# Spreading the softmax with two whole products and a block transposition, contracting two chunks per matmul, loading weight tails from GpSimd, and a remade order

## The chip, the cores and the metric

The kernel runs on one core of one Trainium2 chip, in one launch. The metric is device time in microseconds, the median of several executions: 495.63 us before the change (three runs, 494.08 to 496.65).

A core has five engines with an instruction stream each: TensorE (PE) multiplies matrices, VectorE (DVE), ScalarE (ACT) and GpSimd (POOL) do elementwise work, SyncE (SP) issues transfers. 16 DMA engines move data between HBM and the on-chip SBUF, and they serve the transfers of all issuing engines. Matmuls write to PSUM; from there DVE or ACT copies results to SBUF (an *eviction*).

## What is computed

The reference is a decode step with its gradients. Two tokens (batch 2, one position, width 576) are normalised; a grouped-query attention over a cache of 4096 keys and a gated linear unit are added to the input; then come the gradients of everything.

```python
def _A_ref(x, k_cache, v_cache, wq, wo):          # B=2, D=576, Hq=32, Hkv=16, Sk=4096, Dh=128
    q = (x @ wq).reshape(B, 1, Hq, Dh).transpose(0, 2, 1, 3)
    k, v = repeat(k_cache, 2, axis=1), repeat(v_cache, 2, axis=1)
    p = softmax(einsum("bhqd,bhkd->bhqk", q, k) * Dh ** -0.5)
    o = einsum("bhqk,bhkd->bhqd", p, v)
    return o.transpose(0, 2, 1, 3).reshape(B, 1, Hq * Dh) @ wo

def _B_ref(x, w_gate, w_up, w_down):              # F = 4608
    return ((x @ w_gate) * (x @ w_up)) @ w_down

xn = layernorm(A_x)
out = A_x + _A_ref(xn, k_cache, v_cache, wq, wo) + _B_ref(xn, w_gate, w_up, w_down)
# returned: out and the gradients by A_x, k_cache, v_cache, wq, wo, w_gate, w_up, w_down
```

All arrays are bf16. The two caches are 2 x 16 x 4096 x 128, 32 MiB each (1 MiB for each batch entry and head), and their gradients are as large. The weights are some 25 MB, and their gradients too. So every input is read once, every gradient is written once: 92.48 MB in, 92.48 MB out.

## The kernel before

The work is cut into 16 steps `s`: two key/value heads and one batch entry each. A step loads 2 MiB of keys and 2 MiB of values as tiles of 128 partitions x 8 KB, transposes each on DVE into a tile `X` (four-byte pairs in 32 x 32 blocks), multiplies it with the queries (`score`), takes the softmax, *spreads* the probabilities into two layouts, and uses them twice: for the contraction with the cache (`contract`) and for outer products that are the cache's gradient (`head_outer`), evicted and stored 1 MiB at a time. Values take part with the probabilities `pp`, keys with the gradient of the scores `dd`. Between the steps lie eight groups of `wq`/`wo` columns and nine slices of the gated unit.

Sixteen big tiles of 8 KB per partition serve for everything large; each use has a cap:

```python
NBIG, NGU, NWW, NBD = 16, 1, 5, 3
CAP = {"kv": 9, "X": 7, "st": 4}      # loaded caches, transposed copies, output tiles that wait for their store
KVSTORE = "SP"
```

The order of the instructions is made when the program is built: the class `Order` keeps a clock for every engine and every DMA line, with a written cost for each operation, and issues what can start first, by priority. On the chip each engine then works through its own stream in just that order, waiting on semaphores. So a written cost or a priority does no work on the chip, but it decides the order of the streams, which engine gets an eviction, and which tile is used next.

Spreading, 32 small products of 32 x 32 results each, then one eviction:

```python
def spread(src, dst_ps):
    for c4 in range(4):
        for a in range(4):
            blk, rows = src[:, 32 * c4:32 * c4 + 32], identP[:, 32 * a:32 * a + 32]
            nc.tensor.matmul(dst_ps[32 * a:32 * a + 32, 32 * c4:32 * c4 + 32], lhsT=blk, rhs=rows, ...)
    for a in range(4):
        for c4 in range(4):
            ...                       # the same with lhsT and rhs exchanged, into columns 128 to 255
# in softmax(s), and the same for dd in dscore(s):
spread(c["pr"], m_t[m])
e = yield EV(256)                     # ACT or DVE
cp(e, pp_t[S["pp"]][:].rearrange("p t n -> p (t n)"), m_t[m][:, 0:2 * P])
yield REL("m", m)
```

Contraction, 64 products of 128 columns in four column groups of the array, then a fold:

```python
for part in range(2):
    for k in range(8 * part, 8 * part + 8):
        for j in range(4):
            c, l = k + NCH // 2 * (j // 2), j % 2
            nc.tensor.matmul(ct[32 * j:32 * j + 32, 0:P], lhsT=view(rT, 0, P, 4 * c + 2 * l, [[1, 32]]),
                             rhs=kv_t[kvS[s][t][l]][:, Dh * c:Dh * (c + 1)],
                             start=(k == 0), stop=(k == NCH // 2 - 1))
for l in range(G):
    yield REL("kv", kvS[s][t][l])
...                                   # evict 128 columns to osb, one matmul with fold, copy to oT
```

Outer products: each 1 MiB store needs four evictions of 128 x 1024:

```python
i = yield ACQ("st")                   # an output tile
for k in range(2):
    nc.tensor.matmul(o[:, k, :], lhsT=pr2[32 * c4:32 * c4 + 32, :],
                     rhs=BD[32 * c4:32 * c4 + 32, 8 * l + 4 * h2:8 * l + 4 * h2 + 4, :], ...)
cp(e, view(st[:], 0, P, 2048 * A + 512 * h2, [[1024, 2], [1, 512]]), o[:])
```

The last 64 of the 576 rows of `wq`, `w_gate` and `w_up` (the *tails*) are loaded from SP, whose stream also holds every load of the caches and every store of their gradients:

```python
yield DMA("SP", 0.45, 128 * 256 * 2, 512)
nc.sync.dma_start(ww_t[w][:, 4 * FS:WB], A_wq[512:576, n0:n0 + FS].rearrange("p (h n) -> h p n", h=2))
...
yield DMA("SP", 0.45, 64 * FS * 2, 1024)
nc.sync.dma_start(gu[64 * w:64 * w + 64, 8 * FS:9 * FS], Wsrc[512:576, f0:f0 + FS])
```

Of the kernel before, what the change touches and what calls it, by code (L numbers as in the profile page):

```python
# [13 lines left out]
P = 128  # L14
# [20 lines left out]
class Landing:  # L35
    def __init__(self, work, packet):
        self.work, self.packet, self.t = work, packet, None
# [6 lines left out]
class Lines:  # L44
    def __init__(self):
        self.now, self.line = 0.0, ([], [])

    def run(self, until=None):
        while (self.line[0] or self.line[1]) and (until is None or self.now < until):
            busy = [q for q in self.line if q]  # L50
            total = sum(q[0].packet for q in busy)
            step, first = min(((q[0].work * total / q[0].packet, k) for k, q in enumerate(busy)))
            ends = until is None or step <= until - self.now
            step = step if ends else until - self.now
            for q in busy:
                q[0].work -= step * q[0].packet / total
            self.now += step
            for q in busy:
                if q[0].work < 1e-9 or ends and q is busy[first]:
                    q[0].t = self.now + 1.4  # L60
                    q.pop(0)

    def push(self, k, at, work, packet):
        self.run(at)
        if not (self.line[0] or self.line[1]):
            if at > self.now + 0.3:
                work += DRY
            self.now = max(self.now, at)
        item = Landing(work, packet)
        self.line[k].append(item)  # L70
        now, line, left = self.now, self.line, [[(x, x.work) for x in q] for q in self.line]
        self.line = tuple(list(q) for q in line)
        self.run()
        self.now, self.line = now, line
        for q in left:
            for x, w in q:
                x.work = w
        return item


class Order:

    HOP = 0.12
    def __init__(self):
# [4 lines left out]
        self.quad = None  # L89
# [48 lines left out]
    def start(self, s):  # L138
        r = s.req
        if r[0] == "op":  # L140
            return max(s.ready, self.free[r[1]]), r[1]
# [25 lines left out]
    def run(self):  # L167
        while self.streams:
# [12 lines left out]
            if r[0] in ("op", "any"):  # L181
                cost = r[2] if r[0] == "op" else next(c for x, c, _ in r[1] if x == e)
                quad = r[3] if len(r) > 3 else None
                if quad is not None and self.quad == (1 - quad, t):
                    cost = 0.12
                self.free[e] = t + cost
                if e == "PE":
                    self.quad = (quad, t + cost)
                s.ready = t + cost + self.HOP
# [24 lines left out]
def PE(cost):  # L214
    return ("op", "PE", 0.9 * cost)
# [14 lines left out]
def EV(cols):  # L230
    return ("any", [("ACT", 0.19 + cols * 0.00083, 0.0), ("DVE", 0.16 + cols * 0.00104, cols / 1024 * BIAS)])

# [25 lines left out]
def DMA(engine, cost, nbytes, row=8192):  # L258
# [6 lines left out]
CAP = {"kv": 9, "X": 7, "st": 4}  # L265
MLP0, MLPD = 7, 3.04
KVSTORE = "SP"
WQ0, WO0 = -3, 0
LATENCY, DRY = {"SP": 0.6, "ACT": 0.6, "POOL": 2.0}, 0.4
BIAS = 0.39  # L270
SLACK = {"PE": 0, "ACT": 0.24, "DVE": 0.42, "POOL": 8.48, "SP": 2.18}
STEP = 28.0
HEAD = {"turn0": 32.8, "turn1": 5.6, "att": 18.2, "dsc": -4.1, "con": 20.2, "out1": 32.0, "out0": -0.1, "front": 136.3, "back": 186.6, "W0": -106.9, "W1": 1.4, "load": -18.7}
TAIL = {"turn0": -311.6, "att": -941.4, "dsc": 107.7, "conv": -25.4, "out1": 360.1, "out0": 2.8, "front": 14.6, "back": -0.1, "W0": 72.9, "W1": 0.3, "BD0": -350.1, "load": -45.9}
PR = {"turn0": 159.1, "turn1": 503.5, "att": -177.4, "dsc": -354.1, "conv": 107.5, "con": 255.2, "out1": 239.8, "out0": 221.8,
      "front": -254.4, "back": -141.0, "W0": -80.5, "W1": 16.3, "BD1": 432.8, "BD0": -175.2, "mlp": 0.4, "wout": -413.4,
      "store": 556.3, "load": 796.4, "wload": -183.0, "fin": -239.5, "const": -134.5, "mload": 817.1}
# [8 lines left out]
def kernel(  # L286
# [30 lines left out]
    G = 2  # L317
# [47 lines left out]
    osb_t = tiles("osb", 2, [P, P])  # L365
    od.ring("ch", 2)
    ch_t = []
    for i in range(2):
# [6 lines left out]
            cr=const.tile([P, 1], FP32, name=f"cr{i}"), ds=const.tile([P, P], BF16, name=f"ds{i}")))  # L375
# [66 lines left out]
    fold = const.tile([P, GH], BF16, name="fold")  # L442
    foldf = const.tile([P, GH], FP32, name="foldf")
# [9 lines left out]
    def consts():  # L453
# [17 lines left out]
        yield DVE(0.2)  # L471
        sums(foldf[:].rearrange("p (l r) -> p l r", l=2), [[32, 2], [1, 2], [64, 2]])
# [19 lines left out]
    def front():  # L492
# [23 lines left out]
        yield PE(0.8)  # L516
# [11 lines left out]
        for src, dst in ((yb, dyr), (xnb, xnr)):  # L528
            i = yield ACQ("o")
            o = o_t[i]  # L530
            yield PE(0.6)
# [28 lines left out]
        yield PE(1.0)  # L560
# [52 lines left out]
    def put(engine, parts, tag, slot, events=()):  # L613
        def run():
            for j, (dst, src, nbytes) in enumerate(parts):
                yield DMA(engine, 0.77 if engine == "POOL" else 0.45, nbytes)
# [6 lines left out]
    def unit(mms, pe, cols, ev, store, quad=None):  # L623
        i = yield ACQ("o")
        yield PE(pe) if quad is None else ("op", "PE", pe, quad)
# [6 lines left out]
    def cols_unit(A, rhs, st, off):  # L632
# [10 lines left out]
        return mms, 0.6, 1024, ev  # L643

    def rows_unit(j, lhs, st):
# [10 lines left out]
        return mms, 0.35, D, ev  # L656

    def rows_outer(lhs, dst, p, events=()):
# [3 lines left out]
        store = Store(FC, put("POOL", [(dst, src, 128 * FC * D * 2)], "st", i, events), p)  # L662
# [3 lines left out]
    def cols_outer(rhs, dst, p, events=()):  # L666
# [3 lines left out]
        store = Store(2, put("POOL", [(dst, src, 128 * 4 * FS * 2)], "st", i, events), p)  # L670
# [3 lines left out]
    def tail_outer(rhss, dsts, p, events=()):  # L674
# [4 lines left out]
        store = Store(2, put("POOL", parts, "tl", i, events), p)  # L679

        def mk(A):
# [9 lines left out]
            return mms, 0.3, 256, ev  # L691
# [8 lines left out]
    def mlp(i, Lgu, Ld, gs_slot, wd_slot):  # L700
# [7 lines left out]
        yield PE(1.3)  # L708
# [19 lines left out]
        yield PE(2.2)  # L728
# [30 lines left out]
        yield PE(0.4)  # L759
# [9 lines left out]
        yield PE(0.75)  # L769
# [21 lines left out]
        yield PE(1.5)  # L791
# [17 lines left out]
    def group_front(g):  # L809
# [7 lines left out]
        yield PE(0.75)  # L817
# [12 lines left out]
        def replicate(t):  # L830
            m = yield ACQ("m")
            rp = m_t[m][:, 0:8 * GH].rearrange("p (e k) -> p e k", e=4)
            yield PE(0.35)
# [17 lines left out]
        yield PE(2.2)  # L851
# [18 lines left out]
    def group_back(g):  # L870
# [8 lines left out]
        yield PE(0.4)  # L879
# [15 lines left out]
        yield PE(0.75)  # L895
# [12 lines left out]
        yield PE(0.4)  # L908
# [14 lines left out]
        yield PE(0.8)  # L923
# [27 lines left out]
    def load_kv():  # L951
        n = 0
        for s in range(NS):
            g, b = divmod(s, Bq)
            yield PRIO(pr("load", s))
            for t in range(2):
                for l in range(G):
                    i = yield ACQ("kv")
                    yield DMA("SP", 0.45, 1 << 20)
# [6 lines left out]
    def load_w(item):  # L966
        kind, i = item
        if kind in ("wq", "wo"):
# [3 lines left out]
            if kind == "wq":  # L972
                yield DMA("SP", 0.45, 128 * 256 * 2, 512)
                nc.sync.dma_start(ww_t[w][:, 4 * FS:WB],
                                  A_wq[512:576, n0:n0 + FS].rearrange("p (h n) -> h p n", h=2))
# [10 lines left out]
        else:  # L986
# [4 lines left out]
            for w, Wsrc in enumerate((B_w_gate, B_w_up)):  # L991
# [3 lines left out]
                yield DMA("SP", 0.45, 64 * FS * 2, 1024)  # L995
                nc.sync.dma_start(gu[64 * w:64 * w + 64, 8 * FS:9 * FS], Wsrc[512:576, f0:f0 + FS])
            yield ("lset", Lgu)
            d = yield ACQ("ww")
            yield DMA("SP", 0.45, 128 * FC * D * 2, 4608)
# [40 lines left out]
    def build_BD():  # L1040
        for s in range(NS):
            g, b = divmod(s, Bq)
            for t in (1, 0):
# [5 lines left out]
                yield PE(0.2)  # L1049
# [26 lines left out]
    def spread(src, dst_ps):  # L1076

        for c4 in range(4):
            for a in range(4):
                blk = src[:, 32 * c4:32 * c4 + 32]  # L1080
                rows = identP[:, 32 * a:32 * a + 32]
                nc.tensor.matmul(dst_ps[32 * a:32 * a + 32, 32 * c4:32 * c4 + 32], lhsT=blk, rhs=rows,
                                 start=True, stop=True)
        for a in range(4):
            for c4 in range(4):
                blk = src[:, 32 * c4:32 * c4 + 32]
                rows = identP[:, 32 * a:32 * a + 32]
                nc.tensor.matmul(dst_ps[32 * c4:32 * c4 + 32, P + 32 * a:P + 32 * a + 32], lhsT=rows, rhs=blk,
                                 start=True, stop=True)

    def head_outer(s, t, l, pr2, done):
# [7 lines left out]
        def mk(A, h2):  # L1099
# [9 lines left out]
            return mms, 0.45, 1024, ev  # L1109
# [24 lines left out]
    def softmax(s):  # L1134
# [6 lines left out]
        for l in range(G):  # L1141
            yield PE(0.95)
# [275 lines left out]
```

## Time and profile before

| what | before |
|---|---|
| time, median of 3 runs | 495.63 us |
| span of the profiled execution | 493.5 us |
| busy: PE, DVE, ACT, POOL | 393.3, 362.6, 323.4, 228.2 us |
| moved by DMA | 186.20 MB, mean 377 GB/s |
| share of the 16 DMA engines' time: queue of SP, queue of GpSimd | 71.7%, 23.6% |
| granted TensorE clock, mean | 0.623 of full speed |

How to read it: a *group* of the page is a line of the kernel with one engine and one kind of operands; it has the busy time, the mean duration and the idle time just before its instructions, with what ended that idle time. Lines 392 and 394 are the helper `cp` on ACT and on DVE, line 388 is the helper `t32` (DVE transposition), line 617 issues stores, 960 loads the caches, 974 and 996 load tails, 1070 is `score`, 1082 and 1088 `spread`, 1103 `head_outer`, 1248 `contract`, 1058 builds the block-diagonal operand `BD` on GpSimd. *SPq* is the issuing stream of SP. Stretches are given in us from the span's start.

### The profile page before, as it was taken

The numbers are of one execution on the slowest core, as the hardware profiler recorded it, in microseconds if no ns is written. First come the engines' busy times: TensorE is split into PE (matmuls) and PEld (weight loads), VectorE is DVE, ScalarE is ACT, GpSimd is POOL, SyncE is SP. The second block draws the span as 40 slices with busy tenths as digits, with TensorE's granted clock in tenths as the row PEclk, the third lists the DMA queues.
The fourth block names the chain that finished last, engine by engine and source line by source line (L and its number), as shares of the span: only waits on it lengthen the run. The fifth ranks groups of instructions, "written<-read, shape, count | busy, mean of one in ns | idle before, by whom it ended". The sixth has DMA issues, their size and how long they took to land.

```text
span 493.5 us, 19375 instructions
## 1 busy us (share of the span) xinstructions
PE 393.3 (80%) x8522; PEld 255.6 (52%) x8522; DVE 362.6 (73%) x662; ACT 323.4 (66%) x490; POOL 228.2 (46%) x323
## 2 busy tenths in 40 slices
PE   1549759989888987667799788988878888798886
PEld 0436525556564555545555556546555456455543
DVE  7658848878875797664687788876878498778872
ACT  6027766768746877435587757776828686787682
POOL 6153453619480531327176747350547237472311
PEclk9957755565655579565755766555555566756765
DMA  7999899999999999999999999999999999998864
GB/s 269 403 382 399 307 371 382 419 415 404 360 390 419 373 330 419 410 404 406 348 374 308 408 421 406 388 418 387 346 419 395 419 423 423 400 420 362 320 266 180
DMA packets 34236, 186.20 MB, mean 377 GB/s; under 512 B 4156, under 2 KB 6344, under 8 KB 17768
## 3 DMA queue, kind: packets, MB, share of 16 engines
q1 hardware_dynamic: 22224, 141.25, 71.7%
q0 software_dynamic: 11920, 43.72, 23.6%
q8 instruction: 66, 1.08, 0.8%
q14 instruction: 18, 0.15, 0.1%
q10 hardware_dynamic: 8, 0.00, 0.0%
HBM read 92.48 MB, written 92.48 MB: 375 GB/s over the span
## 4 chain that ended last, share of the span: by engine, by line
PE 40%; DMA 24%; DVE 11%; issue 9%; ACT 8%; POOL 5%; SPq 2%; ACTq 0%; POOLq 0%; DVEq 0%
DMA out_dram<-big 16%; PE ps_o L1103 9%; ACT big L392 7%; PE ps_m L1248 7%; PE ps_m L1070 7%; DMA ww<-in_A_wq_dram 6%; DVE big L388 5%; POOL BD L1058 4%; DVE big L394 3%; DMA ww<-in_A_wo_dram 3%; PE ps_o L651 2%; PE ps_o L637 2%; PE ps_m L854 2%; PE ps_m L731 1%; PE ps_m L595 1%
## 5 line engine op out<-in xcount | busy, mean ns | idle before, releaser
L392 ACT CAST big<-ps_o 128x1024 bf16<-128x1024 f32 (+1 forms) x302 | 271.8, 953 | 63.6 <-PE ps_o L1103 38.4
L388 DVE STREAM_TRANSPOSE big<-big 128x1024 f32<-128x1024 f32 x128 | 155.8, 1228 | 16.8 <-DMA out_dram<-big 8.4
L1058 POOL TENSOR_TENSOR BD<-vr,mask 128x2048 bf16<-128x2048 bf16 x32 | 115.3, 3603 | 65.0 <-DVE vr L394 38.4
L394 DVE CAST big<-ps_o 128x1024 bf16<-128x1024 f32 (+1 forms) x74 | 82.6, 1117 | 17.5 <-PE ps_o L1103 7.4
L1070 PE MATMUL ps_m<-big,W 128*32 128x128 bf16 x2048 | 64.2, 295 | 7.0 <-issue 3.7
L1103 PE MATMUL ps_o<-BD,pp 32*128 32x512 bf16 x256 | 55.5, 536 | 8.2 <-ACT big L392 4.9
L1070 PEld LDWEIGHTS <-W 128*32 128x32 bf16 x2048 | 49.7, 131 | 20.6 <-issue 18.5
L1103 PE MATMUL ps_o<-BD,dd 32*128 32x512 bf16 x256 | 55.2, 535 | 4.6 <-ACT big L392 3.1
L1035 POOL COPY W<-rep 32x16 bf16<-32x16 bf16 x128 | 24.9, 194 | 50.0 <-DVE rep L838 36.6
L617 POOL DMA_DIRECT2D out_dram<-big x43 | 33.1, 771 | 29.8 <-ACT big L392 9.6
L388 DVE STREAM_TRANSPOSE big<-ww 128x1152 f32<-128x1152 f32 x25 | 34.1, 1363 | 8.6 <-DMA ww<-in_A_wo_dram 4.5
L1248 PE MATMUL ps_m<-big,pp 128*32 128x128 bf16 x1024 | 33.7, 304 | 8.3 <-issue 7.0
L1248 PE MATMUL ps_m<-big,dd 128*32 128x128 bf16 x1024 | 31.7, 291 | 6.9 <-issue 5.9
L1248 PEld LDWEIGHTS <-pp 128*32 128x32 bf16 x1024 | 25.1, 137 | 14.8 <-issue 12.7
L1248 PEld LDWEIGHTS <-dd 128*32 128x32 bf16 x1024 | 23.5, 130 | 16.0 <-issue 14.8
L588 POOL COPY wt<-wm 64x128 bf16<-64x128 bf16 (+1 forms) x34 | 9.0, 264 | 40.5 <-DVE wm L582 37.1
L388 DVE STREAM_TRANSPOSE big<-gu 128x1024 f32<-128x1024 f32 x18 | 21.8, 1227 | 7.2 <-issue 6.1
L1103 PEld LDWEIGHTS <-pp 32*128 32x128 bf16 x256 | 11.7, 98 | 23.3 <-issue 20.6
L617 POOL DMA_DIRECT2D out_dram<-tl x26 | 14.5, 561 | 15.6 <-ACT tl L392 15.3
L1103 PEld LDWEIGHTS <-dd 32*128 32x128 bf16 x256 | 12.3, 100 | 18.0 <-issue 14.4
L637 PEld LDWEIGHTS <-xnr 32*128 32x128 bf16 x416 | 15.4, 122 | 8.2 <-issue 7.3
L637 PE MATMUL ps_o<-hb,xnr 32*128 32x128 bf16 x288 | 17.0, 289 | 2.5 <-ACT big L392 1.5
(204 smaller groups left out, 536.0 us busy)
## 6 DMA issues: line engine op xcount, KB each, us to landing
out_dram<-big SPq DMA_DIRECT2D x64, 1024.0 KB, 13.2
big<-in_A_k_cache_dram SPq DMA_DIRECT2D x32, 1024.0 KB, 19.0
big<-in_A_v_cache_dram SPq DMA_DIRECT2D x32, 1024.0 KB, 11.9
out_dram<-big POOLq DMA_DIRECT2D x26, 512.0 KB, 11.8
out_dram<-big POOLq DMA_DIRECT2D x17, 576.0 KB, 9.5
ww<-in_B_w_down_dram SPq DMA_DIRECT2D x9, 576.0 KB, 9.8
ww<-in_A_wo_dram POOLq DMA_DIRECT2D x8, 576.0 KB, 13.7
gu<-in_B_w_gate_dram POOLq DMA_DIRECT2D x9, 512.0 KB, 13.2
```

The source lines that it names most:

```text
L388: nc.vector.transpose(out, in_)
L392: nc.scalar.copy(out, in_)
L394: nc.vector.tensor_copy(out=out, in_=in_)
L617: (nc.gpsimd if engine == "POOL" else nc.sync).dma_start(dst, src)
L637: nc.tensor.matmul(o[:, aa, dc * P:(dc + 1) * P], lhsT=xnr[32 * a:32 * a + 32, dc * P:(dc + 1) * P], rhs=rhs(a), start=True, stop=True)
L651: nc.tensor.matmul(o[:, aa, 0:HD2], lhsT=lhs(a), rhs=dyr[32 * a:32 * a + 32, k * HD2:(k + 1) * HD2], start=True, stop=True)
L854: nc.tensor.matmul(dp, lhsT=Wdy[:, e, 2 * k:2 * k + P], rhs=view(X[:], 0, P, 64 * k + e, [[D, GH], [2, 32]]), start=(k == 0 and e == 0), s ...
L1035: nc.gpsimd.tensor_copy(view(W_t[t][w][:], 32 * a, 32, 6 + 8 * a, [[G * WW, 4], [WW, G], [1, 2]]), view(rep_t[grp[g]["qs"]][:], 32 * a, 32 ...
L1058: nc.gpsimd.tensor_tensor(BD_t[i][:], view(vr_t[v][:], 0, P, 0, [[0, 16], [1, Dh]]), view(mask16[:], 0, P, 0, [[1, 16], [0, Dh]]), ALU.mult)
L1070: nc.tensor.matmul(sc[32 * cq:32 * cq + 32, :], lhsT=view(W[:], 0, P, (be * G + l) * WW + 6 - 4 * c2 - 2 * l, [[1, 32]]), rhs=view(X[:], 0 ...
L1103: nc.tensor.matmul(o[:, k, :], lhsT=pr2[32 * c4:32 * c4 + 32, :], rhs=BD[32 * c4:32 * c4 + 32, 8 * l + 4 * h2:8 * l + 4 * h2 + 4, :], star ...
L1248: nc.tensor.matmul(ct[32 * j:32 * j + 32, 0:P], lhsT=view(rT, 0, P, 4 * c + 2 * l, [[1, 32]]), rhs=kv_t[kvS[s][t][l]][:, Dh * c:Dh * (c + 1)],
```

## The change

Five things are altered; the results stay the same.

1. **Spreading.** Two products of 128 x 128 with the whole permutation matrix take the place of 32 small ones. What lies transposed within each 32 x 32 block is put right by a block transposition on DVE after the eviction, which now writes a tile `sp`.
2. **Contraction.** One product takes two chunks of the cache (256 columns), so 32 take the place of 64. The result has two halves; the eviction has 256 columns, and the fold takes two products. The cache tiles are released when both the contraction and the transposition have read them.
3. **Tails by GpSimd.** The 26 tail loads but the first go to GpSimd's queue.
4. **Caps.** Loaded caches 9 to 10, transposed copies 7 to 4, output tiles 4 to 13, of the same sixteen.
5. **Order.** The written costs of the operations are replaced, and all priorities are set anew. It is for an order that fits the chip better.

```diff
-CAP = {"kv": 9, "X": 7, "st": 4}
-MLP0, MLPD = 7, 3.04
+CAP = {"kv": 10, "X": 4, "st": 13}
+MLP0, MLPD = 2, 6.27
-WQ0, WO0 = -3, 0
-LATENCY, DRY = {"SP": 0.6, "ACT": 0.6, "POOL": 2.0}, 0.4
-BIAS = 0.39
-SLACK = {"PE": 0, "ACT": 0.24, "DVE": 0.42, "POOL": 8.48, "SP": 2.18}
+WQ0, WO0 = -5, -1
+LATENCY, DRY = {"SP": 0.5, "ACT": 0.5, "POOL": 0.57}, 0.4
+CLK = 2.0
+BIAS = 0.75
+SLACK = {"PE": 7.32, "ACT": 0.55, "DVE": 0.31, "POOL": 15.19, "SP": 3.02}
 ...                                  # HEAD, TAIL and PR, the priorities, all new; Lines and Order refined
     def spread(src, dst_ps):
-        for c4 in range(4):
-            for a in range(4):
-                ...                   # 16 products, then 16 more
+        nc.tensor.matmul(dst_ps[:, 0:P], lhsT=identP[:], rhs=src[:], start=True, stop=True)
+        nc.tensor.matmul(dst_ps[:, P:2 * P], lhsT=src[:], rhs=identP[:], start=True, stop=True)
 ...
         spread(c["pr"], m_t[m])
         e = yield EV(256)
-        cp(e, pp_t[S["pp"]][:].rearrange("p t n -> p (t n)"), m_t[m][:, 0:2 * P])
+        cp(e, c["sp"][:], m_t[m][:, 0:2 * P])
         yield REL("m", m)
+        yield DVE(0.4)
+        t32(pp_t[S["pp"]][:].rearrange("p t n -> p (t n)"), c["sp"][:])
 ...                                  # the same for dd
-            for k in range(8 * part, 8 * part + 8):
+            for k in range(8 * part, 8 * part + 8, 2):
                 for j in range(4):
                     c, l = k + NCH // 2 * (j // 2), j % 2
-                    nc.tensor.matmul(ct[32 * j:32 * j + 32, 0:P], lhsT=view(rT, 0, P, 4 * c + 2 * l, [[1, 32]]),
-                                     rhs=kv_t[kvS[s][t][l]][:, Dh * c:Dh * (c + 1)], ...)
-        for l in range(G):
-            yield REL("kv", kvS[s][t][l])
+                    nc.tensor.matmul(ct[32 * j:32 * j + 32, 0:2 * P], lhsT=view(rT, 0, P, 4 * c + 2 * l, [[1, 32]]),
+                                     rhs=kv_t[kvS[s][t][l]][:, Dh * c:Dh * (c + 2)], ...)
+        yield SPAWN(free_kv(s, t), pr("con", s))     # waits for the transposition, then releases
-        nc.tensor.matmul(m_t[m][:, 0:GH], lhsT=osb_t[i][:], rhs=fold[:], start=True, stop=True)
+        for w in range(2):
+            nc.tensor.matmul(m_t[m][:, 0:GH], lhsT=osb_t[i][:, w], rhs=fold[:, w], start=(w == 0), stop=(w == 1))
 ...
-                yield DMA("SP", 0.45, 64 * FS * 2, 1024)
-                nc.sync.dma_start(gu[64 * w:64 * w + 64, 8 * FS:9 * FS], Wsrc[512:576, f0:f0 + FS])
+                yield DMA("POOL", 0.6, 64 * FS * 2, 4096)
+                nc.gpsimd.dma_start(gu[64 * w:64 * w + 64, 8 * FS:9 * FS], Wsrc[512:576, f0:f0 + FS])
```

The tail of `wq` changes in the same way, save for the first group, which stays on SP.

## The prediction

> **What bounds the kernel now.** I read the head of the page first: busy shares, the slices, the DMA queues.
>
> ```profile
> PE 393.3 (80%) x8522; PEld 255.6 (52%) x8522; DVE 362.6 (73%) x662; ACT 323.4 (66%) x490; POOL 228.2 (46%) x323
> DMA  7999899999999999999999999999999999998864
> GB/s 269 403 382 399 307 371 382 419 415 404 360 390 419 373 330 419 410 404 406 348 374 308 408 421 406 388 418 387 346 419 395 419 423 423 400 420 362 320 266 180
> q1 hardware_dynamic: 22224, 141.25, 71.7%
> q0 software_dynamic: 11920, 43.72, 23.6%
> ```
>
> No compute engine is above 80%, and PE's 80% was gathered at a granted clock of 0.623. The DMA engines read 9 in nearly every slice: SP's and GpSimd's queues together hold them for 95.3% of the span. So the kernel is bound by transfers: 186.20 MB, each byte moved once, which no part of the change alters. What can change is the rate. The best slices reach 423 GB/s, and 186.20 MB at 420 would take 443 us; the span is 493.5. Some 50 us lie in slices that move less. The table by stretches (columns: length, busy time of PE, its weight loads, DVE, ACT, POOL, clock, DMA share, GB/s) says where:
>
> ```profile
> 0.00:12.00 12.00, 1.02 (x8) 0.46 (x8) 8.90 (x36) 7.64 (x12) 8.49 (x24) 1.00 0.73 264
> 12.00:440.00 428.00, 350.06 (x7697) 229.08 (x7698) 318.16 (x564) 281.12 (x427) 205.09 (x284) 0.61 1.00 391
> 440.00:494.00 54.00, 42.23 (x821) 26.03 (x816) 35.52 (x63) 34.62 (x52) 14.65 (x16) 0.63 0.74 290
> ```
>
> Head: 3.2 MB in 12 us. Body: 167.3 MB at 391 GB/s. End: 15.7 MB at 290 GB/s with a share of only 0.74, so for about a quarter of 54 us the DMA engines have nothing to do. In 12-us stretches the body is uneven. Fourteen stretches run at 412 to 425 GB/s. Seven lie below 350, such as these two, where the share falls too:
>
> ```profile
> 168.00:180.00 12.00, 10.85 (x295) 7.62 (x296) 10.04 (x16) 7.24 (x11) 8.55 (x17) 0.65 0.87 304
> 252.00:264.00 12.00, 10.94 (x306) 7.99 (x304) 8.26 (x16) 8.98 (x16) 9.27 (x12) 0.50 0.90 343
> ```
>
> Why does the queue run dry? The waits of SP's own stream (us in total, times, longest) name it:
>
> ```profile
> SPq L617 <- ACT big L392: 105.7, 40, 12.4
> SPq L617 <- DVE big L394: 75.3, 19, 11.5
> SPq L960 <- DMA out_dram<-big: 52.6, 10, 11.7
> SPq L996 <- DVE Xt L388: 15.0, 2, 9.7
> SPq L974 <- PE ps_o L651: 10.5, 2, 6.1
> ```
>
> The stream is in order. A store that waits for its eviction holds back the loads behind it; a load waits ten times for an older store that must land before its tile is free; a small tail load that waits for its weight buffer holds back everything behind it, too. Such waits cost nothing while earlier transfers are outstanding, and time once they have drained. The chain of waits agrees: its largest item is DMA out_dram<-big with 15.7% of the span, in seven pieces of 4 to 18 us.
>
> **What the Trainium skill says.** (1) "DMA: Bandwidth & Descriptors", section "Issuing engines are not separate DMA queues": transfers of SP, ACT and GpSimd run on the same 16 engines, and another issuer only saves the sequencer's time. The page agrees that both queues share the 16 engines, so the tails' move brings no bandwidth by itself; here it takes a possible wait out of an in-order stream. (2) The same page, "SWDGE vs HWDGE vs iDMA": a GpSimd packet is preferably up to 4096 bytes. That agrees with 43.72 MB in 11,920 packets, 3.7 KB on average. (3) "TensorE: Matmul & The Clock Gate", Part 1: 107 ns for 128 columns at half clock, about 56 at full, and starts never closer than some 25 ns. The trace agrees: the first contraction's 64 weight loads took 1.63 us, 25 ns each, and its 64 matmuls, four at a time, 1.90 us.
>
> **The change part by part.**
>
> *Contraction.* The groups to be changed:
>
> ```profile
> L1248 PE MATMUL ps_m<-big,pp 128*32 128x128 bf16 x1024 | 33.7, 304 | 8.3 <-issue 7.0
> L1248 PE MATMUL ps_m<-big,dd 128*32 128x128 bf16 x1024 | 31.7, 291 | 6.9 <-issue 5.9
> ```
>
> 65.4 us busy for 32 contractions, 2.04 us each. 2048 products become 1024 with twice the columns, so the streamed columns stay equal. Estimate by the page of (3): 16 rounds of 107 ns, 1.71 us at half clock, before and after; at full clock the 64 starts of 25 ns (1.6 us) give way to 8 rounds of about 107 ns (0.86 us). With half clock in roughly three quarters of the time, 0.2 x 0.75 + 0.8 x 0.25 = 0.35 us each, 11 us of PE in all. Added: 32 evictions of 256 instead of 128 columns (380 against 266 ns on ACT, 3.6 us), and 32 short fold products.
>
> *Spreading.* 1024 small products were 19.6 us busy (lines 1082 and 1088). 64 products of 128 columns remain, at about 0.35 us a pair 11 us: 8 us of PE saved. Added: 32 transpositions of 128 x 256 bf16, 407 ns each in the gT row of the same shape: 13 us of DVE. On the path of one step that is +0.4 us for the transposition and +0.1 for a hop, less 0.1 for fewer products: +0.4 us. Beside transfers it is hidden in every step but the last, +0.4 at the end.
>
> *Balance.* The instruction lists of both programs show the evictions of 128 x 1024: ACT 249 to 266, DVE 59 to 42; those of 576 columns: ACT 53 to 64, DVE 15 to 4. At 1018 and 648 ns, and with wider contraction results and a few more small evictions, ACT goes from 323 to about 355 us; DVE loses 17 x 1.21 + 11 x 0.75 = 29 us and, with 13 gained, ends near 345. PE goes to about 375. All are below 80%: the removed work lies off the path that sets the end, and by itself makes next to nothing of the time.
>
> *Tails.* 25 loads of 64 KB leave SP, whose list has 142 transfers instead of 167; GpSimd issues 119 instead of 94, at some 0.56 us each 14 us more of 228. Of the waits above, 15.0 + 10.5 us stood before such loads. The packets between 512 bytes and 2 KB (6344 - 4156 = 2188) nearly vanish: 1.7 MB, about 4 us of DMA at 391 GB/s; I allow 1 us for larger packets.
>
> *Caps and order.* This is the part that decides. Four output tiles hold 4 MB, and a store needs 13.2 us from issue to landing, so 64 stores can flow, but hardly more than 0.3 MB/us where output is all that is left, as in the last 54 us; there the rate was 290. Thirteen tiles let evictions run ahead of their stores, so SP's stream should wait less for evictions, in the body and above all at the end. In both lists the last load of values stands 9 or 10 big stores before the end, so the work at the end is alike.
>
> **The sum.** Seven body stretches at about 334 GB/s miss (416 - 334) x 12 us = 0.98 MB each, 6.9 MB, 17 us at 400. I take half: -8.5 us. End: 15.7 MB at 325 instead of 290 takes 48.5 us: -5.5. Tails -1, longer chain at the end +0.4. 495.6 - 14.6 = 481; I choose **480 us**. I gain nothing on the stretches with a full share at 390 to 409, since the page doesn't say why they are slower, nor on the first 12 us.
>
> **Rivals.**
> (a) *Hidden anyway.* The order is only moved about, and other waits starve the queue as often: four X tiles instead of seven could make transpositions wait, and loads would wait for tiles held by thirteen outputs. For it: L960 already waits 52.6 us for stores. Then 490 to 500.
> (b) *The order fits far better.* The body at 410 and the end at 350 GB/s: 12 + 408 + 45 = 465 us.
> (c) *An engine becomes the bound in stages.* ACT gets 32 us more work, and GpSimd's stream holds products of 3.6 us (BD) ahead of weight loads. A late weight load or eviction then delays a whole group: 500 or more. Against it: ACT ends near 75%, and evictions are shared with DVE.
>
> **Range and chances.** I hold the middle case for likeliest: the costs written into the order are refined and nothing heavy is added, but a new order can lose in places where the old one did not. Range 464 to 497. Faster by 2% means below 485.7: 0.67. Within 2%: 0.25. Slower: 0.08.
>
> **What would show it.** In the changed profile: body above 400 GB/s and fewer stretches below 350; the last 54 us above 320 GB/s; SP's waits for line 617's evictions well below 181 us and no tail load in its stream; PE near 375, ACT near 355, DVE near 345 us; contraction groups near 54 us together; packets below 2 KB down by some 2000. The prediction fails if the DMA share stays at 0.74 at the end, if L960's waits for stores grow in place of the others, or if the rate at a full share changes.

## The result and the profile after

The changed kernel takes **481.59 us** (median of 4 runs, 480.51 to 484.17) where the kernel before takes 494.87 on the same chip: a ratio of **0.973**, 95% interval 0.968 to 0.978. The profiled executions have spans of 479.3 and 493.5 us.

The head of the page after: busy shares of TensorE and its weight loads, DVE, ACT and POOL; the DMA row in tenths of 40 slices; the rate of each slice.

```profile
PE 379.3 (79%) x6570; PEld 233.1 (49%) x6570; DVE 341.2 (71%) x650; ACT 347.7 (73%) x535; POOL 244.6 (51%) x348
DMA  7999999999999999999999999999999999999685
GB/s 271 382 385 406 386 398 392 402 417 403 363 416 374 330 413 423 382 375 418 419 394 402 412 420 421 410 411 416 420 419 386 415 418 423 411 387 416 241 322 221
q1 hardware_dynamic: 19874, 139.61, 71.5%
q0 software_dynamic: 13504, 45.38, 25.5%
```

No engine reads above 80% here either, and the DMA row is 9 from the second slice to the 37th. It is still a kernel bound by transfers, with fewer gaps in them. The slices at 307 and 308 GB/s have gone; one dip is left in the middle (330, slice 14), and the end.

The table by stretches (length; busy time of PE, its weight loads, DVE, ACT, POOL; clock; DMA share; GB/s):

```profile
12.00:426.00 414.00, 337.06 (x5940) 208.11 (x5944) 300.93 (x548) 301.68 (x469) 218.49 (x317) 0.64 1.01 401
426.00:480.00 54.00, 41.23 (x634) 24.56 (x626) 33.07 (x66) 38.41 (x55) 18.79 (x16) 0.66 0.78 309
```

The body goes from 391 to 401 GB/s: its former 167.3 MB take 417 us at that rate, 11 us less. The last 54 us go from 290 to 309: 15.7 MB take 50.8 us, 3.2 less. Together that is nearly all of the 14.2 us between the spans. In 12-us stretches of the body one is below 350 GB/s (156 to 168 us, 335) where seven were.

Another way to divide it: the queues' shares of 16 engines' time add up to 96.2% before and 97.8% after (SP's, GpSimd's and, with 0.9% and 0.8%, the small ones that fetch instructions and the like). So the DMA engines were idle for 18.8 us of the span and now for 10.5, **8.3 us less idle**, and busy for 474.7 us and now 468.8, **5.9 us less** for nearly the same bytes: while busy they moved 392 GB/s and now 397. So only part of the gain is transfers that no longer stop; another part is transfers that go faster. I use this pair for every kernel below; it is from one profile each and from shares rounded to 0.1%, so a difference of one or two us in it means little.

SP's own stream, by what it waited for (us in total, times, longest):

```profile
SPq L641 <- ACT big L415: 126.3, 37, 9.7
SPq L641 <- DVE big L417: 91.3, 20, 13.5
SPq L984 <- DMA out_dram<-big: 59.1, 13, 11.8
```

This is the surprise: the waits for evictions *rose*, from 181.0 to 217.6 us, and those for older stores from 52.6 to 59.1. And yet the kernel is faster. A wait in SP's stream does no harm while enough earlier transfers are outstanding. The total doesn't show which waits left the DMA engines dry.

### The profile page after: what moved, and what is told of

It is laid out like the page before. It is cut to its first block, busy times and chain, and to the rows that moved or that the text cites. A ratio compares the mean times of both kernels' runs of the same rounds, so it can differ in the third digit from the quotient of the medians.

```text
span 479.3 us, 15470 instructions
## 1 busy us (share of the span) xinstructions
PE 379.3 (79%) x6570; PEld 233.1 (49%) x6570; DVE 341.2 (71%) x650; ACT 347.7 (73%) x535; POOL 244.6 (51%) x348
## 2 busy tenths in 40 slices
DMA packets 33456, 185.98 MB, mean 388 GB/s; under 512 B 5039, under 2 KB 5179, under 8 KB 17003
## 4 chain that ended last, share of the span: by engine, by line
DMA 42%; PE 28%; DVE 11%; ACT 10%; issue 6%; POOL 3%; SPq 0%; POOLq 0%; ACTq 0%; DVEq 0%
DMA out_dram<-big 18%; DMA gu<-in_B_w_up_dram 11%; ACT big L415 8%; DVE big L411 7%; PE ps_m L1094 5%; PE ps_o L1116 5%; DMA big<-in_A_k_cache_dram 5%; PE ps_m L1270 4%; DMA big<-in_A_v_cache_dram 4%; DMA ww<-in_A_wq_dram 3%; PE ps_m L755 2%; PE ps_o L661 1%; PE ps_m L737 1%; POOL BD L1082 1%; PE ps_m L619 1%
## 5 line engine op out<-in xcount | busy, mean ns | idle before, releaser
L415 ACT CAST big<-ps_o 128x1024 bf16<-128x1024 f32 (+1 forms) x330 | 292.6, 961 | 38.2 <-PE ps_o L1116 25.1
L1094 PE MATMUL ps_m<-big,W 128*32 128x128 bf16 x2048 | 58.9, 300 | 4.9 <-DVE big L411 1.2
L417 DVE CAST big<-ps_o 128x1024 bf16<-128x1024 f32 (+1 forms) x46 | 54.0, 1173 | 9.5 <-PE ps_o L1116 8.2
L1116 PE MATMUL ps_o<-BD,dd 32*128 32x512 bf16 x256 | 51.6, 528 | 10.6 <-ACT big L415 7.3
L1116 PE MATMUL ps_o<-BD,pp 32*128 32x512 bf16 x256 | 51.0, 529 | 6.9 <-POOL BD L1082 3.3
L641 POOL DMA_DIRECT2D out_dram<-big x43 | 33.3, 774 | 40.4 <-ACT big L415 22.7
L1270 PE MATMUL ps_m<-big,pp 128*32 128x256 bf16 x512 | 29.6, 390 | 4.4 <-DVE pp L411 3.1
L1270 PE MATMUL ps_m<-big,dd 128*32 128x256 bf16 x512 | 27.9, 360 | 1.8 <-DVE rep L862 0.7
L1270 PEld LDWEIGHTS <-pp 128*32 128x32 bf16 x512 | 15.9, 129 | 13.1 <-DVE pp L411 6.0
L1116 PEld LDWEIGHTS <-dd 32*128 32x128 bf16 x256 | 11.7, 99 | 21.5 <-issue 17.6
L415 ACT CAST sp<-ps_m 128x256 bf16<-128x256 f32 x29 | 11.1, 382 | 15.1 <-PE ps_m L1102 14.1
L737 PE MATMUL ps_m<-gu,xs 128*32 128x128 bf16 x360 | 10.8, 282 | 12.1 <-DMA gu<-in_B_w_up_dram 10.0
## 6 DMA issues: line engine op xcount, KB each, us to landing
big<-in_A_v_cache_dram SPq DMA_DIRECT2D x32, 1024.0 KB, 15.5
```

Of the source, the lines that this page charges most:

```text
L415: nc.scalar.copy(out, in_)
L417: nc.vector.tensor_copy(out=out, in_=in_)
L641: (nc.gpsimd if engine == "POOL" else nc.sync).dma_start(dst, src)
L737: nc.tensor.matmul(ug[32 * a:32 * a + 32, 1 - w, :], lhsT=xs[:, dc if dc < 4 else 4 + w, :], rhs=gu[:, FS * k + P * a:FS * k + P * (a + 1) ...
L1094: nc.tensor.matmul(sc[32 * cq:32 * cq + 32, :], lhsT=view(W[:], 0, P, (be * G + l) * WW + 6 - 4 * c2 - 2 * l, [[1, 32]]), rhs=view(X[:], 0 ...
L1270: nc.tensor.matmul(ct[32 * j:32 * j + 32, 0:2 * P], lhsT=view(rT, 0, P, 4 * c + 2 * l, [[1, 32]]), rhs=kv_t[kvS[s][t][l]][:, Dh * c:Dh * ( ...
```

## The experiments

Three theories were open. The expectations below call them A, C and B, in this order; D is the theory that an order made for other durations and waits runs dry more often.

- **T1, order (A):** the gain is the new order with its caps; operations and tails weigh nothing, being off the path.
- **T2, tails (C):** it is the tails' leaving SP's in-order stream.
- **T3, operations (B):** it is the new spreading and contraction, through work that the view of busy time doesn't show as critical.

Order (with its caps), place of the tails and operations can be switched one by one, which gives eight kernels. Two are known.

### The six mixed kernels

**order_alone:** the changed kernel with the old operations and the tails issued by SP, each at the place in the order that it has in the changed kernel.

```diff
 # changed kernel
-        nc.tensor.matmul(dst_ps[:, 0:P], lhsT=identP[:], rhs=src[:], start=True, stop=True)
+        ...                           # old spread, 32 products; old contract, 64; no transposition from sp
-                (nc.gpsimd if i else nc.sync).dma_start(ww_t[w][:, 4 * FS:WB],
+                nc.sync.dma_start(ww_t[w][:, 4 * FS:WB],
-                nc.gpsimd.dma_start(gu[64 * w:64 * w + 64, 8 * FS:9 * FS], ...)
+                nc.sync.dma_start(gu[64 * w:64 * w + 64, 8 * FS:9 * FS], ...)
```

> The kernel after with the old spreading, the old contraction and the tails on SP, all in the new order and with the new caps: only the order and the caps differ from the kernel before. Theory A (order and caps fill the transfer queue, the operations lie off the path): 481 to 486 us, DMA share of the body at 1.01. Theory B (the shorter TensorE work makes the gain): 490 us or more. Theory C (tails out of SP's stream make it): 488 us or more, with SP waits of over 20 us at the tail loads.

**after_oldops:** only the first half of that edit, so tails on GpSimd. **after_tails_sp:** only the second half.

> The kernel after with the old spreading and contraction alone, in the same order of instructions. Theory A: within 2 us of the kernel after, 480 to 484 us. Theory B: 488 us or more. Theory C: as A.

> The kernel after with the tail loads issued by SP again, each at its place in the same order. Theory A: 481 to 485 us; theory B the same. Theory C: 487 us or more, since a tail load that waits for the one gate/up buffer stops SP's loads and stores.

**ops_tails_old_order, before_newops, before_tails_pool:** the kernel before, with the new operations and the tails on GpSimd, with the operations alone, and with the tails alone:

```diff
 # kernel before
-                nc.sync.dma_start(ww_t[w][:, 4 * FS:WB],
+                (nc.gpsimd if i else nc.sync).dma_start(ww_t[w][:, 4 * FS:WB],
-                nc.sync.dma_start(gu[64 * w:64 * w + 64, 8 * FS:9 * FS], ...)
+                nc.gpsimd.dma_start(gu[64 * w:64 * w + 64, 8 * FS:9 * FS], ...)
```

> The kernel before with the new spreading, the new contraction and the tails on GpSimd, in the old order and with the old caps. Theory A: 491 to 496 us, PE busy down by some 15 us without effect. Theory B: 483 to 488 us. Theory C: 485 to 489 us, with the low stretches near 170 and 257 us gone.

> The kernel before with the new spreading and contraction alone, in the old order. With tails moved too the old order took 500.6 us. Theory D (a stream made for other durations and other waits runs dry more often, whatever was made cheaper): slower than before or equal, 495 to 500 us, though PE's busy time falls by some 15 us. Theory B (less TensorE work is worth 5 us by itself, as its removal cost in the new order): 488 to 491 us.

> The kernel before with the tail loads issued by GpSimd alone, in the old order. Theory C (tails out of SP's stream are worth 7 us by themselves, as their return cost in the new order): 486 to 490 us. Theory D: 494 to 499 us.

All eight, with ratios to the kernel before on the same chip, and the idle and busy time of the DMA engines from each profile:

| order, caps | tails | operations | kernel | us | ratio (95%) | DMA idle, us | DMA busy, us |
|---|---|---|---|---|---|---|---|
| old | SP | old | before | 494.9 | 1 | 18.8 | 474.7 |
| old | SP | new | before_newops | 489.7 | 0.990 (0.986 to 0.994) | 19.2 | 472.6 |
| old | GpSimd | old | before_tails_pool | 509.8 | 1.031 (1.027 to 1.034) | 25.4 | 481.6 |
| old | GpSimd | new | ops_tails_old_order | 500.6 | 1.011 (1.007 to 1.015) | 21.5 | 478.0 |
| new | SP | old | order_alone | 496.1 | 1.003 (1.001 to 1.005) | 22.7 | 470.9 |
| new | SP | new | after_tails_sp | 488.7 | 0.989 (0.986 to 0.992) | 22.0 | 465.8 |
| new | GpSimd | old | after_oldops | 487.2 | 0.986 (0.982 to 0.989) | 13.1 | 471.4 |
| new | GpSimd | new | after | 481.6 | 0.973 (0.968 to 0.978) | 10.5 | 468.8 |

The profiled execution of before_newops was its slowest, 493.6 us, so its two last figures are high by some 4 us together.

Each part can be read in four pairs of rows. *Operations*: -5.2, -9.2, -7.4, -5.6 us, a gain everywhere. *Tails to GpSimd*: +14.9 and +10.9 in the old order, -8.9 and -7.1 in the new. *Order*: +1.2 and -1.0 with the tails on SP, -22.6 and -19.0 with the tails on GpSimd.

So T1 and T2 fall as they stand: neither the order nor the move of the tails gains anything by itself. **The gain is in the pair**, about 8 us with either form of the operations; the priorities of the new order were set with the tails on GpSimd. Beside it T3 holds for 5 to 9 us. Few of the ranges above were met: B's for before_newops and C's for after_tails_sp held, order_alone lies in B's and C's (its tail loads wait 52 us in SP's stream), after_oldops falls between A's and B's, and for ops_tails_old_order and before_tails_pool every range was too low.

The last two columns divide the gains differently. The new order shortens the DMA engines' busy time by 4 to 10 us in all four pairs, the new operations by 2 to 5. Why the same transfers then take less time is open.

Where a misplaced tail loses its time can be followed in after_tails_sp, which has the same operations and the same order as the changed kernel. Three stretches of it, and the same three of the changed kernel after them:

```profile
24.00:36.00 12.00, 0.58 (x10) 0.39 (x6) 2.73 (x5) 0.90 (x3) 1.08 (x6) 0.58 1.02 393
48.00:60.00 12.00, 11.30 (x161) 7.91 (x161) 8.27 (x15) 9.20 (x16) 4.88 (x10) 0.50 0.55 225
60.00:72.00 12.00, 9.40 (x234) 5.96 (x232) 10.34 (x20) 9.57 (x14) 7.08 (x12) 0.78 0.71 238
```

```profile
24.00:36.00 12.00, 8.45 (x149) 5.23 (x149) 10.93 (x20) 7.64 (x14) 7.95 (x11) 0.71 1.02 385
48.00:60.00 12.00, 7.41 (x155) 4.76 (x155) 6.86 (x12) 7.30 (x12) 4.89 (x8) 0.64 0.96 384
60.00:72.00 12.00, 10.86 (x206) 7.03 (x206) 9.27 (x20) 6.07 (x11) 8.45 (x14) 0.58 1.01 399
```

The second number from the end is the DMA share: 0.55 and 0.71 against 0.96 and 1.01. (384 - 225 + 399 - 238) x 12 us is 3.8 MB not moved, 9.6 us at 400 GB/s, which covers all of the 7.1 us that this kernel loses. The hole begins with the first stretch: from 24 to 36 us the transfers run, but all four engines stand nearly still. The timelines show what for. First after_tails_sp, then the changed kernel; line 998 issues the tail of `wq`, line 845 computes with it:

```profile
7.93 0.54 SPq L998 DMA_DIRECT2D ww<-in_A_wq_dram  x1
36.41 0.59 PE L845 MATMUL ps_m<-xs,ww 128*128 128x2 bf16 x16 [11.24 <-DMA ww<-in_A_wq_dram]
```

```profile
3.52 0.86 POOL L998 DMA_DIRECT2D ww<-in_A_wq_dram  x1
24.84 0.64 PE L845 MATMUL ps_m<-xs,ww 128*128 128x2 bf16 x20
```

On SP the 64 KB of the second group's tail are issued behind the eight 1 MiB loads of the caches with which SP's stream begins. In the trace the tail's packets move only from 33.6 to 35.6 us, after those eight loads, 26 to 28 us after the issue. TensorE waits 11.2 us for them, and the other engines for TensorE. On GpSimd's own queue the tail has less ahead of it, and the products start at 24.84 us with no wait in the profile. The first store of a gradient then leaves SP at 45.9 us where it left at 34.2, the loads behind the stores are late as well, and the DMA engines run dry. order_alone has the same wait of TensorE (11.8 us) and the same hole in the same slices (237 and 288 GB/s). In the second half of the hole SP adds a wait of its own, before the next group's tail, whose buffer is still being read by the products of line 661:

```profile
SPq L998 <- PE ps_o L661: 5.2, 1, 5.2
```

That is the wait which the prediction had named, a small load that holds back the large ones. SP stands 45.8 us before tails in this kernel, in 13 waits, but from 72 us to the end of the body no slice falls under 368 GB/s. So more of the harm runs the other way: the large loads hold back a small one that an engine needs, and the hole is 12 us old when SP comes to its own wait. The kernels differ in nothing but the tails' queue, so the hole is theirs; that this one load is the whole of the 7.1 us was not tested by a run that moves it alone.

The opposite case, before_tails_pool: the stretches 252 to 264 and 264 to 276 us fall from 343 and 332 to 296 and 320 GB/s, and the wait of transpositions for a tile whose store must land grows from 11.0 to 26.7 us:

```profile
DVE big L388 <- DMA out_dram<-big: 26.7, 12, 11.4
```

Perhaps the tails no longer slow SP's stream where the old order counted on it, so that stores and loads meet for tiles at other times. No run shows this, and which single meeting costs most was not isolated.

**before_wqtail_pool:** the kernel before with only the seven `wq` tails on GpSimd, to see whether few or many of them do the harm.

> The kernel before with the seven wq tails alone on GpSimd, the eighteen gate and up tails still on SP, in the old order. All 25 moved cost 15 us (509.8). If the cost is that of the gated unit's data, which then lands late for a TensorE stream made for an earlier landing, 493 to 497 us here. If it is the order of SP's stream that loses its brake, or GpSimd's time, a third to a half of it: 499 to 504 us.

Measured: 499.24 us, ratio 1.009 (1.005 to 1.013): 4 of the 15 us, with 7 of the 25 loads; the second expectation held. So the harm doesn't come from the `wq` tails alone; most of it comes only when the other 18, those of `w_gate` and `w_up`, move too.

### The caps without an order made for them

```diff
 # after_oldcaps: changed kernel            # before_newcaps: kernel before
-CAP = {"kv": 10, "X": 4, "st": 13}         -CAP = {"kv": 9, "X": 7, "st": 4}
+CAP = {"kv": 9, "X": 7, "st": 4}           +CAP = {"kv": 10, "X": 4, "st": 13}
```

The order is remade by each kernel's own costs and priorities. In after_oldcaps three of the 32 block transpositions then read the `sp` tile after the step's other spread wrote it, and in before_newcaps some of the 32 operands `BD` are built from a later group's queries: those results are computed from other data, with the same work and the same transfers.

> The kernel after with the old caps (9, 7, 4), for which the order is made again with the new costs and priorities. At most 4 output tiles are then in use at once, against 7 in the kernel after. Theory A (room for outputs ahead of their stores is what helps): 487 to 492 us, last 54 us below 295 GB/s. Otherwise 480 to 484 us.

> The kernel before with the new caps (10, 4, 13) and its old costs and priorities; the order is made again, with up to 7 output tiles in use. Theory A: 486 to 491 us. Theory D: the priorities were found for the old caps, so 494 us or more.

Measured: after_oldcaps 497.44 us, ratio 1.005 (1.003 to 1.007); before_newcaps 529.24 us, ratio 1.066 (1.061 to 1.071). With four output tiles the changed kernel loses 16 us; with thirteen, the kernel before loses 34. after_oldcaps lies above both of its ranges, though its last 54 us run at 268 GB/s, as theory A had it; for before_newcaps theory D held. Thirteen tiles are thus no help in themselves: under the old priorities the DMA engines are idle for 46.4 us. It is not that loads wait more for output tiles, since SP's waits for older stores fall from 52.6 to 29.9 us; the tails of `wq` alone now wait 34.2 us for their buffer. Both runs change caps and order together, so what the caps are worth in an order made for them stays open. In the built order of the changed kernel seven output tiles are in use at most, not thirteen.

### Which operation: spreading or contraction

**after_oldspread:** the changed kernel with the old 32-product spreading, in the same order.

```diff
-        nc.tensor.matmul(dst_ps[:, 0:P], lhsT=identP[:], rhs=src[:], start=True, stop=True)
-        nc.tensor.matmul(dst_ps[:, P:2 * P], lhsT=src[:], rhs=identP[:], start=True, stop=True)
+        ...                           # the 32 small products
-        cp(e, c["sp"][:], m_t[m][:, 0:2 * P])
-        t32(pp_t[S["pp"]][:].rearrange("p t n -> p (t n)"), c["sp"][:])
+        cp(e, pp_t[S["pp"]][:].rearrange("p t n -> p (t n)"), m_t[m][:, 0:2 * P])
```

> The kernel after with the old spreading alone (32 small products, no block transposition), in the same order; the contraction stays new. Old spreading and contraction together cost 5.6 us (487.2 against 481.6). If the contraction carries the gain, 481 to 483 us; if the spreading does, 485 to 488 us; if they share it by their savings of TensorE time (8 to 11), 483 to 485 us.

**after_halfcon:** the changed kernel with every second contraction product left out; half of the keys are then missing from the attention output and from the gradient by the queries.

```diff
-            for k in range(8 * part, 8 * part + 8, 2):
+            for k in range(8 * part, 8 * part + 8, 4):
```

> The kernel after with every second product of the contraction left out (16 of 32, so half the keys are missing from the attention's output and from the queries' gradient), in the same order; transfers and evictions unchanged. TensorE loses some 28 us of busy time. Theory A (TensorE off the path): 480 to 482 us. Theory B (its time counts, because it is full in stretches although 79% on average; 14 us of it were worth 5 to 7 us): 472 to 477 us.

Measured: after_oldspread 485.29 us (482.02 to 486.15), ratio 0.979 (0.974 to 0.983); after_halfcon 481.50 us (480.06 to 483.41), ratio 0.972 (0.968 to 0.976). Going back to the old spreading costs 3.7 us; going on to the old contraction as well (after_oldops) costs 1.9 more. Only the sum of 5.6 is clear of the noise: the interval of after_oldspread overlaps with that of the changed kernel (0.968 to 0.978) and with that of after_oldops. Halving the new contraction gains nothing. **Less contraction is worth nothing here; the larger part of the 5.6 us seems to go with the spreading.**

after_halfcon also shows why a saving on PE isn't what its count says. The groups of the contraction, line 1270, and of the outer products, line 1116, which are the same in both kernels, in the changed kernel and then in after_halfcon:

```profile
L1270 PE MATMUL ps_m<-big,pp 128*32 128x256 bf16 x512 | 29.6, 390 | 4.4 <-DVE pp L411 3.1
L1270 PE MATMUL ps_m<-big,dd 128*32 128x256 bf16 x512 | 27.9, 360 | 1.8 <-DVE rep L862 0.7
L1116 PE MATMUL ps_o<-BD,dd 32*128 32x512 bf16 x256 | 51.6, 528 | 10.6 <-ACT big L415 7.3
L1116 PE MATMUL ps_o<-BD,pp 32*128 32x512 bf16 x256 | 51.0, 529 | 6.9 <-POOL BD L1082 3.3
```

```profile
L1270 PE MATMUL ps_m<-big,pp 128*32 128x256 bf16 x256 | 17.8, 399 | 6.2 <-DVE pp L411 4.9
L1270 PE MATMUL ps_m<-big,dd 128*32 128x256 bf16 x256 | 18.5, 387 | 1.6 <-DVE rep L862 0.7
L1116 PE MATMUL ps_o<-BD,dd 32*128 32x512 bf16 x256 | 57.2, 580 | 6.7 <-ACT big L415 5.8
L1116 PE MATMUL ps_o<-BD,pp 32*128 32x512 bf16 x256 | 55.4, 575 | 8.9 <-POOL BD L1082 6.3
```

The mean of one outer product rises from 528 to 578 ns. The contraction groups fell by 21.2 us (57.5 to 36.3), yet PE as a whole is busy 376.2 instead of 379.3 us: the granted clock is 0.594 instead of 0.648, and the other products take longer. All executions agree on the clock: it is 0.594 to 0.634 in the six of after_halfcon and 0.648 to 0.676 in the four of the changed kernel. So this run doesn't decide between its two theories: PE's time hardly fell, and whether a real saving of it would count is open.

Is it the spreading's shorter way to the probabilities? The timelines of the first step say no. Columns: start, length, operation. The changed kernel, then after_oldspread:

```profile
25.91 0.27 PE L1101 MATMUL ps_m<-pr,identP 128*128 128x128 bf16 x1 [0.35 <-ACT vr L415]
26.32 0.37 ACT L415 CAST sp<-ps_m 128x256 bf16<-128x256 f32 x1 [0.46 <-PE ps_m L1102]
27.37 0.40 DVE L411 STREAM_TRANSPOSE pp<-sp 128x256 bf16<-128x256 bf16 x1
27.83 0.62 PE L1270 MATMUL ps_m<-big,pp 128*32 128x256 bf16 x8 [1.55 <-DVE pp L411]
```

```profile
26.32 0.28 PE L1106 MATMUL ps_m<-identP,pr 128*32 128x32 bf16 x16 [0.35 <-ACT vr L415]
26.80 0.37 ACT L415 CAST pp<-ps_m 128x256 bf16<-128x256 f32 x1 [0.53 <-PE ps_m L1112]
27.23 1.26 PE L1279 MATMUL ps_m<-big,pp 128*32 128x256 bf16 x20 [0.53 <-ACT pp L415]
```

From the first product to the first contraction product 1.92 us pass in the new form and 0.91 in the old. The block transposition stands behind a large one on DVE, so in this step the new way is a microsecond *longer*. Nor does PE's busy time show it: 376.2 us with the old spreading and 379.3 with the new, at profiled clocks of 0.665 and 0.648. The loss is idle time of the DMA engines, 15.5 against 10.5 us, in two places: between 144 and 168 us the rate is 326 with the old spreading and 352 with the new, and in each kernel's own last 54 us it is 288 and 309. With the old one, SP waits 8.9 us for older stores in the first of these places, with the new one 2.9. Why 30 fewer small products per spread lead to that is **open**; it may be the 960 fewer products and weight loads that PE's stream has to work through, or only that streams meet differently.

### A new order for the changed kernel

The pair of order and tails matters by 20 us, so a better order may be there. **after_neworder** is the changed kernel with its priorities searched anew by the kernel's own build-time clock; the same caps, transfers and operations.

```diff
-MLP0, MLPD = 2, 6.27
+MLP0, MLPD = 6, 5.9
-WQ0, WO0 = -5, -1
+WQ0, WO0 = -15, -29
-BIAS = 0.75
+BIAS = 0.99
 ...                                  # SLACK, HEAD, TAIL and PR all new; dd spreads through a tile sq of its own
```

> The changed kernel with all priorities searched anew (PR, HEAD, TAIL, SLACK, BIAS, MLP0, MLPD, WQ0 and WO0), same caps, same operations, same written costs, same transfers; dd gets a spreading tile of its own beside that of pp, so that any order is free. Main theory (engine work is off the path; what is left to gain is the order of the in-order streams, and the build-time clock can tell a better order from a worse one): 470 to 478 us, with the end above 330 GB/s or the stretches below 350 GB/s gone. Rival (the order of the changed kernel is about as good as this clock can find, its errors are larger than what is left): 480 to 490 us, with dry stretches in other places. The third (fit of order hardly matters, the rate of DMA does): within 2 us of 481.6.

Measured: 497.96 us (493.69 to 502.1), ratio 1.003 (1.001 to 1.006). All three expectations failed: by the ratios it is some 15 us slower than the changed kernel. Its slices and SP's longest sum of waits:

```profile
GB/s 275 385 373 421 419 314 404 411 413 407 409 400 322 345 389 401 419 395 375 393 424 420 418 406 392 406 324 276 389 409 426 420 414 416 376 292 265 326 289 243
SPq L640 <- ACT big L414: 171.0, 45, 16.2
```

Holes at 314, 322, 324 and 276 GB/s, an end of 267 GB/s over 54 us (share 0.72), and 23.3 us of idle DMA. The longest wait of SP for an eviction is 16.2 us where it was 13.5. The lesson holds: order is worth some 15 us with the same operations and transfers. But here the build-time clock led to the worse of two orders, so no version here beats the changed kernel.

## Why the prediction was right, and where its steps were not

The total was right, 480 us for 481.6, and so was the outer frame: bound by transfers, no engine above 80%. That the gain comes only where the DMA queue runs dry was half of it: 8.3 us are less idle time, but 5.9 us are shorter busy time of the DMA engines. The prediction gained nothing on the rate at a full share and named a change of it as a sign against itself; the sign came. By its steps:

- **Body and end.** Predicted -8.5 us for the body and -5.5 for the end; by the stretches -11 and -3.2. The body passed 400 GB/s and its slow stretches went from seven to one. The end reached 309 GB/s, not 325, and its share only 0.78: in the chain of waits it is still computation after the last load of values (landed at 442 us) that sets it.
- **SP's waits for evictions "well below 181 us": wrong.** They are 217.6. The picture of thirteen tiles that let evictions run ahead fails with it: seven are in use, and thirteen tiles under the old priorities cost 34 us.
- **"Caps and order is the part that decides": half right.** Order with caps by themselves changed the time by +1.2 us (order_alone). With the tails on GpSimd they are worth -19 to -23 us. The step left out that an order and the queue of each transfer are one decision.
- **Tails, -1 us: mis-sized.** The packets between 512 bytes and 2 KB fell by 2048, as said, but those under 512 bytes rose by 883 (4156 to 5039), and in the new order the DMA engines were busy 3 us *longer* with the tails on GpSimd (468.8 us) than on SP (465.8). The gain is 7 us, all from less idle time (22.0 to 10.5). I had read the 15.0 + 10.5 us of waits before tails in the profile and given them no term of the sum; what I hadn't asked is when a tail lands that stands behind large loads in SP's queue, and which engine waits for it (11.2 us in after_tails_sp). The Trainium skill, "DMA: Bandwidth & Descriptors", section "Issuing engines are not separate DMA queues", is borne out on the bandwidth: another issuer brought none. It also says that another issuer saves only the sequencer's time; here it changed when the load landed, and the measurement decides.
- **Operations "make next to nothing of the time": wrong in size.** They gain 5 to 9 us in every combination, and in the changed order more of it seems to go with the spreading than with the contraction. For less contraction the step's result was right: half of it left out changes nothing, though PE's time hardly fell with it.
- **Engines.** Predicted PE 375, ACT 355, DVE 345, contraction 54 us; measured 379.3, 347.7, 341.2 and 57.5. In the same order the new contraction saves 4.8 us of PE (62.4 us in after_oldops, 57.6 in after_oldspread), not 11. PE's estimate took the clock as given. The small block transpositions were close, 433 and 426 ns where 407 was taken.

So the right total is partly luck: too much for caps and order alone, too little for tails and operations. By the way before, order_alone, after_oldops, after, the measured terms are +1.2, -8.9 and -5.6 us; the predicted ones -14 (order), -1 (tails) and +0.4 (operations). The terms depend on the way: with the operations first, then the tails and the order last, they are -5.2, +10.9 and -19.0. No way gives the predicted ones.

## What to carry to other kernels

In a kernel bound by transfers with in-order streams, the order and the engine that issues each transfer are one choice: change one alone and a good part can turn into a loss as large, so test parts in both surroundings before calling one useless or useful. For each small load ask what stands ahead of it in its queue and who waits for it. Judge such a kernel by the idle and the busy time of the DMA engines together and by the stretches where the idle time lies; the total of the issuing engine's waits can rise while the kernel gets faster. A build-time model that led to a good order can lead to a worse one on the next search, as here: which of two orders is better, the chip has to say.

## What the runs showed of the hardware

- **Less matmul work, lower granted clock.** Leaving out 21 us of contraction took the mean clock of the profiled execution from 0.648 to 0.594, and PE stayed busy for 376 of 379 us; over all executions the clocks are 0.594 to 0.634 against 0.648 to 0.676. It isn't so with every change of the work: with the old spreading, 960 products more, the mean over six executions is 0.657, as in the changed kernel.
- **A small load lands after the large ones ahead of it in its queue.** 64 KB issued by SP behind eight loads of 1 MiB moved 26 to 28 us after the issue (after_tails_sp).
- **Over 400 GB/s held for 414 us**, in the body of the changed kernel, which reads and writes half and half over the whole run.
- **Other operations and another order changed how long the DMA engines were busy.** The same transfers took 470.9 us of DMA time in order_alone and 465.8 in after_tails_sp, which differ in the engines' operations alone; in all four such pairs the new operations take 2 to 5 us less, of which the fetches of instructions explain at most about one (0.8% and 0.7% of the time before and after). One profile each, cause not found.
